# The main stage's list is made with durations, ways and one transfer queue read from a trace

## The chip, the core and the metric

The kernel runs on one core of one Trainium2 chip. The metric is device time in microseconds (us) of that core; a kernel's time is the median of its runs. TensorE is PE, VectorE is DVE, ScalarE is ACT, GpSimd is POOL; SyncE is SP, which here only issues transfers (ACT issues some as well). Two clocks occur for TensorE, 2.4 GHz (granted share 1.00) and 1.2 GHz (0.50).

## What is computed

Three layers follow each other: a decayed linear attention, a mixture of eight experts whose weights come from eight rounds of row and column normalisation, and a bilinear block. The two last make up the main stage.

```python
# x: (3072, 384), from the attention
P = np.exp(x @ w_gate - max)
for _ in range(8):
    P /= P.sum(1, keepdims=True) + 1e-09
    P /= P.sum(0, keepdims=True) + 1e-09
    P *= N / E
for e in range(8):
    out += P[:, e:e+1] * (np.maximum(x @ w1[e], 0.0) @ w2[e])   # w1[e]: 384x1024
y = ((out @ w_a) * (out @ w_b)) @ w_out                         # w_a: 384x1536
```

## The kernel before

Every float32 operand of a matmul is split into a high and a low part, and a product is three matmuls (high by high, high by low, low by high). The kernel has two stages, each with its own list of operations. The first (attention, the first expert for most rows) ends about 421 us into the span and is not touched. The second, the main stage, goes in six phases: three for the experts and three for the bilinear block, each with 1024 rows of `x`.

A phase is a row of *jobs*. The front of a job multiplies by the first weight, in a scheme with 15 products of sums instead of 18 plain ones: each is one group of three 128x512 matmuls (line 998) into a PSUM bank of `pG` (two banks) or `pF` (three banks). ACT copies a bank out to a buffer `z` ("keep"), or DVE adds or subtracts it into a `z`; there are 19 such buffers, handed out in turn while the program is written, so that the same operation always has the same buffer, in both kernels. ACT and POOL or DVE then make the high and low parts into `er`. The back of a job multiplies these by the second weight (line 368, 128x384 matmuls, 3 or 6 in an operation, three banks `pR`), and DVE adds each result into `acc`.

Beside this stand transfers: weights already split come back in three pieces (`w<-wfmoe`, `w<-wfout`), go out once as a whole (1920 KB, `wfmoe<-w`, `wfout<-w`), and `er<-w2d` brings the second weight. The 64-bit weights of the bilinear block are converted on DVE in seven small operations (lines 311 to 319) and written out by ACT (`wd<-z`, line 968). Where an expert phase ends, `acc` is transposed on PE (line 1126), copied to `z`, and written out by ACT (`x2d<-z`).

What sets the order of the instructions is a list scheduler, the class `Plan`. Each operation is added with a priority, an engine, a cost in us, and the buffers that it reads and writes. `Plan.order` lets time pass: each engine in turn takes, of the operations whose inputs are reckoned ready, the one with the lowest priority number; PE first prefers the kind (512 or 384 columns) that it has, until it has stayed `STAY` us with it. What is ready is reckoned so: the cost of the producer, and then, to another engine, a fixed gap (0.4 us here, 1.5 us to SP; 0.13 us on the same engine), and for a transfer a fixed `late` (3 us for a store, 5 us for a load). No transfer waits for another in this reckoning. The result is an order for each engine, which the chip follows strictly: an engine stands still until the next instruction's inputs are there. A POOL operation and those DVE operations that are marked "+" share a port in the list.

Of the kernel before, what the change touches and what calls it, by code (L numbers as in the profile page):

```python
# [84 lines left out]
class Plan:  # L85
# [11 lines left out]
    SWITCH = .02  # L97

    def __init__(self, gap=GAP, hold=GAP, same=SAME, over=0.0, ranked=False, early=0, slack=None, port=False, stay=0.0):
        self.port, self.shared, self.stay, self.kind = port, set(), stay, {}  # L100
        self.ranked, self.early, self.slack = ranked, early, slack or gap
        self.gap, self.hold, self.same, self.over = gap, hold, same, over
        self.ops = []
        self.last = {}

    def add(self, prio, eng, cost, reads, writes, fn, late=0.0, fill=False, kind=0):
        n = len(self.ops)
        self.kind[n] = kind
        if self.port and eng in ("POOL", "DVE+"):
            self.shared.add(n)  # L110
        eng = eng.rstrip("+")
        cost -= self.over if eng in ("DVE", "ACT") else 0.0
        deps = set()
        for key in reads:
            w, r = self.last.setdefault(key, (None, []))
            if w is not None:
                deps.add(w)
            r.append(n)
        for key in writes:
            w, r = self.last.get(key, (None, []))  # L120
            deps.update(x for x in r if x != n)
            if w is not None:
                deps.add(w)
            self.last[key] = (n, [])
        self.ops.append((prio, eng, cost, deps, fn, late, fill))
# [5 lines left out]
    def order(self, share):  # L131
# [67 lines left out]
                    todo.setdefault(self.ops[u][1], []).append(u)  # L199
        return made  # L200


@with_exitstack
def kernel(
# [36 lines left out]
    S_COST, X_COST = (.1, .0026), .9  # L241
    LATER = 8.0
    LATER_PE = 600
    STAY = 1.2
    SPREAD = 2000
    W_STEP = SPREAD // 3
    LAG = 100
# [39 lines left out]
    xd = [spill.tile([KD, 128, NT], F32, name=f"x{n}d") for n in (1, 2)]  # L287
# [14 lines left out]
    count = {"raw": 0, "h": 0, "w2": 0, "l": 0}  # L302
# [120 lines left out]
    PE, DVE, ACT, POOL, SP = "PE", "DVE", "ACT", "POOL", "SP"  # L423
    plan = Plan(same=.1, over=.07, ranked=True, early=2000, slack=.8)
# [503 lines left out]
    TPG = 2 * TB // 128  # L928
    plan = Plan(.4, 1.5, port=True, stay=STAY)
    used.update(F=0, R=0)  # L930
# [232 lines left out]
    for n, (ph, u, blocks, ab) in enumerate(jobs):  # L1163
        kind, g = phases[ph]
        base = n - u
        if u == 0:
            if ph:
                more = l_of + (stage_of if ph != 3 else []) + (raw_of if ph not in (1, 3) else [])
# [19 lines left out]
        end = n + 1 == len(jobs) or jobs[n + 1][0] != ph  # L1188
# [10 lines left out]
            first = False  # L1199
    assert not later  # L1200
    with tc.manual_schedule():
        for fn in plan.order(0.0):
            fn()  # L1203


# [38 lines left out]
```

## Time and profile before

| what | value |
|---|---|
| median of 3 runs | 2188.34 us (2185.81 to 2189.74) |
| profiled execution, its own time | 2187.57 us |
| its span in the profile | 2185.8 us |
| PE busy | 2159.0 us (99%) |
| DVE, ACT, POOL busy | 1610.4, 942.2, 910.4 us |
| granted clock, mean | 0.998 |

A matmul's record reaches from its start to the modelled end of its last column, and the next one starts before that: a busy PE is therefore one that always has the next matmul, not one at its peak. What PE can lose is read from its waits, from the granted clock, and from the distance between the starts of matmuls.

### The profile page before, as it was taken

What the parts mean: (1) busy time and instruction counts of PE and PEld (TensorE: products, weight loads), DVE (VectorE), ACT (ScalarE), POOL (GpSimd) and SP (SyncE); (2) the same over time, 40 slices, a digit from 0 to 9 for tenths busy, and PEclk for the clock granted to TensorE, in tenths of its full rate; (3) what the DMA queues carried; (4) which work ended last, traced back from release to release, by engine and by line L of the source; (5) the groups of instructions that cost most, each with busy time, mean ns of one, the idle gap of its engine ahead of it and who ended that gap; (6) DMA issues with size and microseconds to landing.
All of it is one profiled execution on the core that took longest, in us unless ns stands there. A gap on an engine that the chain in (4) does not pass through costs nothing.

```text
span 2185.8 us, 41932 instructions
## 1 busy us (share of the span) xinstructions
PE 2159.0 (99%) x15933; PEld 1961.6 (90%) x15933; DVE 1610.4 (74%) x2888; ACT 942.2 (43%) x1779; POOL 910.4 (42%) x924
## 2 busy tenths in 40 slices
PE   8999999999999999999999999999999999999999
PEld 8999999989999999898999988999999888888888
DVE  7878888387878778676787697677776866866755
ACT  3544454454444445433334344433343545533331
POOL 2212121378876664431222255433222577634322
PEclk9999999999999999999999999999999999999999
DMA  6556653456765558875454466666443555787552
GB/s 138 112 118 147 174 122 80 140 201 214 253 245 188 208 187 302 288 250 186 141 173 157 158 225 235 219 218 215 165 163 127 185 203 193 283 284 255 173 173 73
DMA packets 318346, 413.43 MB, mean 189 GB/s; under 512 B 146880, under 2 KB 207936, under 8 KB 314688
## 3 DMA queue, kind: packets, MB, share of 16 engines
q1 hardware_dynamic: 302832, 393.97, 56.0%
q10 hardware_dynamic: 15312, 16.78, 2.2%
q8 instruction: 125, 2.05, 0.4%
q14 instruction: 77, 0.63, 0.1%
HBM read 279.33 MB, written 126.62 MB: 186 GB/s over the span
## 4 chain that ended last, share of the span: by engine, by line
PE 93%; DVE 3%; DMA 2%; SPq 1%; ACT 0%; issue 0%; POOL 0%; ACTq 0%; DVEq 0%
PE pR L368 39%; PE pG L998 27%; PE pF L998 10%; PE pM L356 4%; PE pM L368 3%; PE pT L482 1%; PE pA L525 1%; PE pO L638 1%; PE pA L537 1%; PE pO L610 1%; PE pA L569 1%; PE pO L644 1%; PE pA L580 1%; DVE z L1203 1%; PE pO L682 1%; PE pM L729 0%
## 5 line engine op out<-in xcount | busy, mean ns | idle before, releaser
L368 PE MATMUL pR<-er 128*128 128x384 f32 x5052 | 976.2, 336 | 2.9 <-DVE acc L1203 2.7
L368 PEld LDWEIGHTS pR<-er 128*128 128x128 f32 x5052 | 897.9, 188 | 55.2 <-DVE acc L1203 3.0
L1203 POOL TENSOR_TENSOR er<-z,er 128x512 fp32r<-128x512 f32 x221 | 299.3, 1367 | 659.6 <-ACT er L1203 512.8
L1203 ACT ACTIVATE z<-pG 128x512 f32<-128x512 f32 x474 | 282.8, 599 | 658.6 <-PE pG L998 578.2
L1203 DVE SCALAR_TENSOR_TENSOR acc<-pR,prob,acc 128x384 f32<-128x384 f32 x504 | 305.2, 612 | 194.4 <-PE pR L368 192.8
L998 PE MATMUL pG<-xsh,w 128*128 128x512 f32 x1134 | 431.4, 394 | 5.9 <-ACT z L1203 5.8
L1203 ACT ACTIVATE er<-z 128x512 fp32r<-128x512 f32 x420 | 248.8, 625 | 143.4 <-PE pR L368 107.9
L1203 DVE TENSOR_TENSOR z<-pF,z 128x512 f32<-128x512 f32 x324 | 221.3, 687 | 93.6 <-PE pF L998 70.3
L998 PE MATMUL pG<-er,w 128*128 128x512 f32 x972 | 278.8, 395 | 1.2 <-DVE z L1203 0.8
L998 PEld LDWEIGHTS pG<-xsh,w 128*128 128x128 f32 x1134 | 212.7, 188 | 42.1 <-ACT z L1203 8.1
L1203 DVE TENSOR_TENSOR z<-z,pG 128x512 f32<-128x512 f32 x243 | 166.2, 685 | 84.7 <-PE pG L998 81.2
L998 PE MATMUL pG<-xsl,w 128*128 128x512 f32 x567 | 223.8, 395 | 0.0
L998 PEld LDWEIGHTS pG<-er,w 128*128 128x128 f32 x972 | 180.0, 188 | 32.8 <-DVE z L1203 3.7
L708 POOL TENSOR_TENSOR er<-l,er 128x256 fp32r<-128x256 f32 x84 | 71.7, 854 | 281.0 <-ACT l L706 249.5
L1203 DVE SCALAR_TENSOR_TENSOR er<-z,er 128x512 fp32r<-128x512 f32 x171 | 171.6, 1014 | 6.2 <-ACT er L1203 5.2
L1203 POOL TENSOR_TENSOR stage<-stage 128x128 f32<-128x128 f32 x325 | 158.9, 521 | 38.9 <-DMA stage<-in_moe_w_dram 28.9
L1203 DVE TENSOR_TENSOR z<-pG,z 128x512 f32<-128x512 f32 x174 | 119.9, 689 | 67.3 <-PE pG L998 64.5
L1203 POOL TENSOR_TENSOR w<-stage,w 128x768 fp32r<-128x768 f32 (+2 forms) x75 | 124.1, 1662 | 43.4 <-ACT w L1203 38.8
L998 PE MATMUL pF<-er,w 128*128 128x512 f32 x486 | 139.0, 394 | 1.4 <-DVE z L1203 1.4
L326 POOL TENSOR_TENSOR er<-raw,er 128x384 fp32r<-128x384 f32 (+1 forms) x82 | 94.5, 1157 | 98.5 <-ACT er L324 84.6
L998 PE MATMUL pF<-xsh,w 128*128 128x512 f32 x324 | 126.9, 393 | 0.0
L998 PEld LDWEIGHTS pG<-xsl,w 128*128 128x128 f32 x567 | 106.3, 188 | 10.7
(166 smaller groups left out, 2594.2 us busy)
## 6 DMA issues: line engine op xcount, KB each, us to landing
er<-w2d SPq DMA_DIRECT2D x138, 384.0 KB, 4.5
wfmoe<-w SPq DMA_DIRECT2D x19, 1920.0 KB, 7.8
w<-wfmoe SPq DMA_DIRECT2D x38, 768.0 KB, 5.2
w2d<-er SPq DMA_DIRECT2D x69, 384.0 KB, 4.0
w<-wfmoe SPq DMA_DIRECT2D x38, 640.0 KB, 4.9
w<-wfmoe SPq DMA_DIRECT2D x38, 512.0 KB, 4.3
wfout<-w SPq DMA_DIRECT2D x8, 1920.0 KB, 7.5
raw<-in_moe_w_dram SPq DMA_DIRECT2D x64, 192.0 KB, 2.9
```

The source lines that it names most:

```text
L326: plan.add(prio + 1, "POOL", S_COST[0] + m * S_COST[1], [gk, key], [key], lambda: nc.gpsimd.tensor_tensor(out=lj, in0=got, in1=f32(hj), op ...
L356: nc.tensor.matmul(out=ps, lhsT=a[:, kk, fs], rhs=b[:, kk, :], start=(i == 0), stop=(i == 3 * KD - 1),)
L368: nc.tensor.matmul(out=ps, lhsT=a[:, off:off + 128], rhs=b, start=(start and i == 0), stop=(stop and i == n - 1))
L482: nc.tensor.transpose(ps[0:R, p * 128:p * 128 + 128], src[:, p * 128:p * 128 + R], ident)
L525: nc.tensor.matmul(out=A0[o:o + 64, w, :], lhsT=pct(bk)[r, g, :], rhs=pct(bq)[r, g, :])
L537: nc.tensor.matmul(out=A1[o:o + 56, 0, w, :].rearrange("j (b e) -> j b e", e=8), lhsT=pct(k3)[r, g, 0:56], rhs=qv[r, g, :, 1, :])
L569: nc.tensor.matmul(out=A1[o:o + 48, 1, w, :].rearrange("j (b e) -> j b e", e=16), lhsT=pct(k3)[r, g, 0:48], rhs=qv[r, g, :, 1, :])
L580: nc.tensor.matmul(out=A1[o:o + 32, 0, w, :], lhsT=pct(k3)[r, g, 0:32], rhs=pct(q3)[r, g, 32:64])
L610: nc.tensor.matmul(out=ps[64 * hd:64 * hd + m, p * D:(p + 1) * D], lhsT=kn[64 * c:64 * c + 64, p * R + 64 * hd:p * R + 64 * hd + m], rhs=b ...
L708: op(POOL, .76, [f"hh{ft}", kf], [f"hl{ft}"], lambda hh=hh, hl=hl, hf=hf: nc.gpsimd.tensor_tensor(out=hl, in0=hf, in1=f32(hh), op=ALU.subt ...
L998: nc.tensor.matmul(out=ps, lhsT=a[:, slot], rhs=b, start=(new and i == 0), stop=(i == 2), skip_group_check=not new)
L1203: fn()
```

## The change

A second scheduler, `Plan.timed`, makes the main stage's list. It picks as `order` does, but counts with tables: `TAKES` has for each engine and reckoned cost the distance from start to start, `COLUMNS` and `AFTER` that of a matmul by its columns and its place in a run, `WAY` the way from each engine to the next one. Transfers from SP and ACT go through one queue, by bytes. `STAY` goes from 1.2 to 1.8. No operation is added or taken out, and the buffers of each stay the same. The list is called as `plan.timed(.03, .3)`: 0.03 us on top of each way, 0.3 us on top of a landing.

```diff
-    STAY = 1.2
+    STAY = 1.8
-        for fn in plan.order(0.0):
+        for fn in plan.timed(.03, .3):
             fn()
+    WAY = {"PE": .205, "DVE": .115, "ACT": .125, "POOL": .085}
+    COLUMNS = {512: .2267, 384: .1733, 256: .12}
+    AFTER = {512: (3.7, 6.7, 6.7, -1.2, 4.2, 8.7, 2.5, 5.0, 3.3, 0.0), 384: (-2.5, 3.7, 6.2, 2.5, 3.7, .8, 0.0),
+        "DVE": {.62: .528, .56: .467, .68: .602, .69: .603, .7: .603, .93: .91, 1.0: 1.016, .204: .22, .255: .28, .3: .24, .383: .3},
+        "ACT": {.6: .52, .45: .387, .49: .387, .521: .414, .612: .53, .737: .635, .863: .735, .37: .263, .47: .395, .25: .27},
+    DMA_WAY, DMA_RATE, DMA_PIECE = 1.93, 400e3, .001
+    def moves(self, n):
+        _, eng, cost, _, _, late, _ = self.ops[n]
+        key, cost, kb = self.key[n], round(cost, 3), 1024
+        if eng == "ACT":
+            return (256 * kb, 128) if key[:2] == "xd" else (128 * kb, 128)
+        if cost == .45:
+            return (1920 * kb, 128) if key[:2] == "wf" else (128 * kb * {"0": 6, "1": 4, "2": 5}[key[-1]], 256)
...
+            at, eng = best
+            n = min((n for n in todo[eng] if ready[n] <= at + 1e-9),
+                    key=lambda n: (eng == "PE" and (self.kind[n] == now) != (run < self.stay), prio[n]))
+            todo[eng].remove(n)
+            cost, late = round(self.ops[n][2], 3), self.ops[n][5]
+            if n in self.shared:
+                at = max(at, port - .03)
...
+                for _ in range(count):
+                    takes += self.COLUMNS[cols] + .001 * more[min(place, len(more) - 1)]
+                    place += 1
+            else:
+                takes = self.TAKES.get(eng, {}).get(cost, cost)
...
+            if n in self.shared:
+                port = max(port, at + takes)
...
+            free[eng] = end = at + takes
+            made.append(self.ops[n][4])
+            dma = eng == "SP" or (eng == "ACT" and late > 0)
+            if dma:
+                size, pieces = self.moves(n)
+                queue = max(end + self.DMA_WAY - .03, queue) + size / self.DMA_RATE + pieces * self.DMA_PIECE
+                end = queue + .03
+            for u in users[n]:
+                to = self.ops[u][1]
+                way = 0.0 if dma or (eng == to and eng != "SP") else self.WAY.get(eng, 0.0) + near
+                ready[u] = max(ready[u], end + way + (far if dma or to == "SP" else 0.0))
```

The lists differ on every engine, but most operations move by a few places. Three of them are needed below.

**Place 1, ACT** (some 1029 us into the span before): the store of a converted piece, `wd0_104<-z7_6478`, and the next operation that overwrites the same buffer `z7`. Before:

```order
L1203 ACTIVATE er_92<-z8_6479 128x512
L1203 ACTIVATE er_92<-z2_6473 128x512
L1203 ACTIVATE er_92<-z5_6476 128x512
L968 DMA wd0_104<-z7_6478 128x256
L1203 ACTIVATE z7_6478<-pG1_6464 128x512
L1203 ACTIVATE z11_6482<-pG0_6463 128x512
```

And now:

```order
L1065 DMA wd0_104<-z7_6478 128x256
L1300 ACTIVATE z6_6477<-pG0_6463 128x512
L1300 ACTIVATE er_92<-z8_6479 128x512
L1300 ACTIVATE er_92<-z2_6473 128x512
L1300 ACTIVATE er_92<-z5_6476 128x512
L1300 ACTIVATE z1_6472<-pG0_6463 128x512
L1300 ACTIVATE z17_6488<-z17_6488 128x512
L1300 ACTIVATE z12_6483<-pG0_6463 128x512
L1300 ACTIVATE z0_6471<-z0_6471 128x512
L1300 ACTIVATE er_92<-z17_6488 128x512
L1300 ACTIVATE er_92<-z15_6486 128x512
L1300 ACTIVATE z14_6485<-pG0_6463 128x512
```

The store stood right ahead of the operation that overwrites its source; now eleven activations stand between, and `z11` and then `z7` come behind the last of these rows.

**Place 2, PE**, at the same time: the matmuls ahead of the `pG` product of job parts `xsh_6496`, which needs the bank that `z11` is copied from. Before:

```order
L998 MATMUL pF_6467<-er,w_84 128x512 x3
L368 MATMUL pR_6468<-er 128x384 x6
L368 MATMUL pR_6469<-er 128x384 x6
L998 MATMUL pF_6465<-xsh_80,w_85 128x512
L998 MATMUL pF_6465<-xsl_81,w_85 128x512
L998 MATMUL pF_6465<-xsh_80,w_85 128x512
L998 MATMUL pF_6467<-er,w_84 128x512 x3
L368 MATMUL pR_6470<-er 128x384 x6
L368 MATMUL pR_6468<-er 128x384 x6
L998 MATMUL pG_6463<-xsh_6496,w_84 128x512
```

And now:

```order
L1095 MATMUL pG_6463<-xsh_6494,w_84 128x512
L1095 MATMUL pG_6463<-xsl_6495,w_84 128x512
L1095 MATMUL pG_6463<-xsh_6494,w_84 128x512
L1095 MATMUL pG_6464<-xsh_74,w_85 128x512
L1095 MATMUL pG_6464<-xsl_75,w_85 128x512
L1095 MATMUL pG_6464<-xsh_74,w_85 128x512
L1095 MATMUL pF_6467<-er,w_84 128x512 x3
L465 MATMUL pR_6470<-er 128x384 x6
L465 MATMUL pR_6468<-er 128x384 x6
L1095 MATMUL pG_6463<-xsh_6496,w_84 128x512
```

A run of six matmuls with 512 columns has become one of nine. Over the main stage the 3645 matmuls with 512 columns stand in 514 runs (593 before), most of six or nine, and the 5010 with 384 columns in 502 (577 before).

**Place 3, ACT**, some 1793 us into the span before: the three stores of transposed rows at the end of the third phase, and the operations that overwrite `z8`, `z2` and `z4` again. Before:

```order
L1203 DMA x2d_97<-z8_6479 128x512
L1203 DMA x2d_97<-z2_6473 128x512
L1203 ACTIVATE z4_6475<-pR1_6469 128x512
L1203 ACTIVATE w10_84<-stage_86 128x640
L1203 DMA x2d_97<-z4_6475 128x512
L1203 ACTIVATE er_92<-z0_6471 128x512
L1203 ACTIVATE er_92<-z12_6483 128x512
L1203 ACTIVATE z8_6479<-pG1_6464 128x512
L1203 ACTIVATE z4_6475<-pG0_6463 128x512
L1203 ACTIVATE z2_6473<-pG1_6464 128x512
```

And now:

```order
L1300 DMA x2d_97<-z8_6479 128x512
L1300 ACTIVATE z2_6473<-pR0_6468 128x512
L1300 DMA x2d_97<-z2_6473 128x512
L1300 ACTIVATE z4_6475<-pR1_6469 128x512
L1300 DMA x2d_97<-z4_6475 128x512
L1300 ACTIVATE er_92<-raw0_87 128x384
L1300 ACTIVATE w10_84<-stage_86 128x640
L1300 ACTIVATE er_92<-z0_6471 128x512
L1300 ACTIVATE z8_6479<-pG1_6464 128x512
L1300 ACTIVATE z2_6473<-pG1_6464 128x512
L1300 ACTIVATE z4_6475<-pG0_6463 128x512
```

The store of `z8` goes out one activation earlier, and `z4`, the last to be stored, is now overwritten last.

## Rows read from the trace of the kernel before

**Rows 1.** The page: engine share, and the costliest group (mean ns behind the comma).

```profile
PE   2159.0 (99%) x15933; PEld 1961.6 (90%) x15933; DVE 1610.4 (74%) x2888; ACT 942.2 (43%) x1779; POOL 910.4 (42%) x924
...
L368 PE MATMUL pR<-er 128*128 128x384 f32 x5052 | 976.2, 336 | 2.9 <-DVE acc L1203 2.7
```

**Rows 2.** PE's waits from 421 us on: total us, times, longest.

```profile
PE pG L998 <- ACT z L1203: 5.8, 4, 2.0
PE pR L368 <- DVE acc L1203: 2.7, 1, 2.7
PE pR L1126 <- DVE acc L1203: 2.5, 2, 1.9
PE pF L998 <- DVE z L1203: 1.4, 1, 1.4
PE pR L778 <- DVE prob L769: 1.2, 2, 1.0
PE pG L998 <- DVE z L1203: 0.8, 3, 0.5
PE pR L356 <- ACT l L722: 0.3, 1, 0.3
PE pG L998 <- DVE er L1203: 0.3, 1, 0.3
PE pR L368 <- ACT acc L1203: 0.2, 1, 0.2
```

**Rows 3.** Windows behind two waits: PE, PEld, DVE, ACT, POOL busy, PEclk, DMA share, GB/s.

```profile
1037.30:1042.00 4.70, 4.65 (x16) 4.38 (x17) 1.93 (x4) 2.15 (x4) 2.59 (x2) 0.66 0.26 96
...
1284.70:1288.00 3.30, 3.22 (x8) 2.79 (x9) 2.13 (x5) 0.63 (x1) 0.62 (x1) 0.50 0.57 193
```

**Rows 4.** Timeline, 1026 to 1039 us: start, us, engine, line, tiles; idle time in brackets.

```profile
1026.31 0.52 SPq L1203 DMA_DIRECT2D w<-wfmoe  x1
...
1028.37 0.39 PE L998 MATMUL pG<-xsh,w 128*128 128x512 f32 x1
...
1028.78 0.34 ACTq L968 DMA_DIRECT2D wd<-z  x1
...
1029.76 2.25 PE L368 MATMUL pR<-er 128*128 128x384 f32 x12
...
1031.85 0.39 PE L998 MATMUL pF<-xsh,w 128*128 128x512 f32 x1
...
1033.23 2.25 PE L368 MATMUL pR<-er 128*128 128x384 f32 x12
...
1036.21 1.08 ACT L1203 ACTIVATE z<-pG 128x512 f32<-128x512 f32 x2 [8.22 <-DVE acc L1203]
...
1037.35 0.50 PE L998 MATMUL pG<-xsh,w 128*128 128x512 f32 x1 [1.86 <-ACT z L1203]
```

**Rows 5.** The chain that ended last, 1020 to 1045 us, its longest piece.

```profile
1028.78 7.34 DMA wd<-z
```

**Rows 6.** Timeline, 1790 to 1808 us.

```profile
1793.25 0.43 SPq L1203 DMA_DIRECT2D wfout<-w  x1
...
1793.53 0.81 ACTq L1203 DMA_DIRECT2D x2d<-z  x2
...
1801.13 0.60 ACT L1203 ACTIVATE z<-pG 128x512 f32<-128x512 f32 x1 [4.09 <-DMA x2d<-z]
...
1801.78 0.50 PE L998 MATMUL pG<-xsh,w 128*128 128x512 f32 x1 [2.01 <-ACT z L1203]
...
1805.59 0.50 PE L998 MATMUL pG<-xsh,w 128*128 128x512 f32 x1 [1.26 <-ACT z L1203]
```

**Rows 7.** Transfers by line: issues, KB each, median us to landing.

```profile
wfout<-w SPq DMA_DIRECT2D x8, 1920.0 KB, 7.5
...
wd<-z ACTq DMA_DIRECT2D x36, 128.0 KB, 2.7
x2d<-z ACTq DMA_DIRECT2D x18, 256.0 KB, 5.7
```

**Rows 8.** Timeline, 1274 to 1287 us.

```profile
1281.54 1.39 DVE L317 TENSOR_TENSOR z<-z 128x256 f32<-128x256 f32 x1
...
1284.12 0.60 DVE L1203 SCALAR_TENSOR_TENSOR acc<-pR,prob,acc 128x384 f32<-128x384 f32 x1
...
1284.78 1.33 PE L368 MATMUL pR<-er 128*128 128x384 f32 x3 [2.66 <-DVE acc L1203]
```

More of the change, by code (lines that the diff above doesn't have):

```diff
@@ L99, in __init__ @@
     def __init__(self, gap=GAP, hold=GAP, same=SAME, over=0.0, ranked=False, early=0, slack=None, port=False, stay=0.0):
-        self.port, self.shared, self.stay, self.kind = port, set(), stay, {}
+        self.port, self.shared, self.stay, self.kind, self.key = port, set(), stay, {}, {}
         self.ranked, self.early, self.slack = ranked, early, slack or gap
@@ L108, in add @@
         self.kind[n] = kind
+        self.key[n] = next(iter(writes), "")
         if self.port and eng in ("POOL", "DVE+"):
@@ L200, in order @@
         return made
+    ENGINES = ("PE", "DVE", "ACT", "POOL", "SP", "clock")
+    WAY = {"PE": .205, "DVE": .115, "ACT": .125, "POOL": .085}
+    RUNS = {.681: (512, 3), 1.362: (512, 6), .522: (384, 3), 1.044: (384, 6), .53: (384, 3), 1.06: (384, 6),
+            .36: (256, 3), .72: (256, 6), 1.08: (256, 9)}
+    COLUMNS = {512: .2267, 384: .1733, 256: .12}
+    AFTER = {512: (3.7, 6.7, 6.7, -1.2, 4.2, 8.7, 2.5, 5.0, 3.3, 0.0), 384: (-2.5, 3.7, 6.2, 2.5, 3.7, .8, 0.0),
+             256: (2.0,), "pause": (6.0, 6.2, 3.3, 7.5, 3.3, 2.5, 2.5, 2.0, 0.0)}
@@ new lines @@
+    TAKES = {
+        "PE": {.2: .117, .33: .245, .35: .2, .69: .713},
+        "DVE": {.62: .528, .56: .467, .68: .602, .69: .603, .7: .603, .93: .91, 1.0: 1.016, .204: .22, .255: .28, .3: .24, .383: .3},
+        "ACT": {.6: .52, .45: .387, .49: .387, .521: .414, .612: .53, .737: .635, .863: .735, .37: .263, .47: .395, .25: .27},
+        "POOL": {.46: .417, 1.026: .977, 1.252: 1.256, 1.29: 1.256, 1.54: 1.522, 1.828: 1.81, .76: .72},
+        "SP": {.36: .46, .38: .47, .4: .42, .42: .4, .45: .615, 1.2: 1.23, 2.4: 2.5},
+    }
@@ new lines @@
+    DMA_WAY, DMA_RATE, DMA_PIECE = 1.93, 400e3, .001
[6 more added lines that the diff above has]
+            return (1920 * kb, 128) if key[:2] == "wf" else (128 * kb * {"0": 6, "1": 4, "2": 5}[key[-1]], 256)
+        if cost == .38:
+            return 384 * kb, 128
+        if key[:2] == "pb":
+            return 256 * kb, 512
+        return (256 * kb if cost == .4 and key[:2] != "sg" else 192 * kb), 128
@@ new lines, in timed @@
+    def timed(self, near, far, shift={}):
+        left, users, ready = [], [[] for _ in self.ops], [0.0] * len(self.ops)
+        todo = {eng: [] for eng in self.ENGINES}
+        prio = [o[0] + shift.get(n, 0) for n, o in enumerate(self.ops)]
+        for n, o in enumerate(self.ops):
+            left.append(len(o[3]))
+            for d in o[3]:
+                users[d].append(n)
+            if not o[3]:
+                todo[o[1]].append(n)
+        free, port, queue, run, now, made = dict.fromkeys(self.ENGINES, 0.0), 0.0, 0.0, 0.0, 0, []
+        width, place, paused = 0, 0, False
+        while any(todo.values()):
+            best = None
+            for eng, ns in todo.items():
+                if ns:
+                    soon = min(ready[n] for n in ns)
+                    at = soon if eng == "clock" else max(free[eng], soon)
+                    if best is None or at < best[0]:
+                        best = (at, eng)
+            at, eng = best
[5 more added lines that the diff above has]
+                at = max(at, port - .03)
+            if eng == "PE" and cost in self.RUNS:
+                cols, count = self.RUNS[cost]
+                if width != cols:
+                    width, place, paused = cols, 0, False
+                if at > free["PE"] + .04:
+                    place, paused = 0, True
+                more = self.AFTER["pause" if paused else cols]
+                takes = 0.0
+                for _ in range(count):
[3 more added lines that the diff above has]
+                takes = self.TAKES.get(eng, {}).get(cost, cost)
+                if eng == "ACT" and late and cost == .45:
+                    takes = .42
+                if eng == "PE":
+                    width, place, paused = 0, 0, False
+            if n in self.shared:
+                port = max(port, at + takes)
+            if self.kind[n]:
+                run = takes + (run if self.kind[n] == now else 0.0)
+                now = self.kind[n]
+            free[eng] = end = at + takes
[9 more added lines that the diff above has]
+                ready[u] = max(ready[u], end + way + (far if dma or to == "SP" else 0.0))
+                left[u] -= 1
+                if not left[u]:
+                    todo[to].append(u)
+        return made
```

## Prediction

> **What bounds it now.** I first read the engine shares: PE is busy for 99% of the span [rows 1], and no other engine for more than 74%. So the main stage ends when PE has got through its matmuls, and a change of order can win or lose three things only: PE's waits, its clock, and the distance between its starts.
>
> I read the waits next, for the main stage alone [rows 2]. The nine rows add up to 5.8 + 2.7 + 2.5 + 1.4 + 1.2 + 0.8 + 0.3 + 0.3 + 0.2 = 15.2 us, in 16 waits. Few, then, and long: there is no steady shortage, but single places where the list was mistaken. A wait costs more than its row shows, since it is counted from the end of a matmul's record. A 384-column record lasts 0.336 us on average [rows 1], while 12 such matmuls go from 1029.76 to 1031.85, that is 0.174 us each [rows 4]. So a wait costs another 0.16 us, 2.6 us over 16.
>
> Third, the clock. Behind two waits, of 1.86 and 2.66 us, there is a stretch at a lower grant: 0.66 on average over 4.70 us, and 0.50 (the 1.2 GHz level) over 3.30 us [rows 3]. That is 4.70 x 0.34 + 3.30 x 0.50 = 3.25 us lost.
>
> In all 15.2 + 2.6 + 3.25 = 21 us hang on waits: 1% of the time, and the most that better order can return there.
>
> **The hops.** The old list adds 0.4 us for every way to another engine. At 1801.13 ACT takes 0.60 us, and PE starts at 1801.78, 0.05 us behind [rows 6]: 0.65 us, where the old list counts 0.6 + 0.4 = 1.0, and the new one 0.52 + 0.125 + 0.03 = 0.675. DVE's `acc` at 1284.12 takes 0.60, and PE starts 0.06 us behind it [rows 8]; the old list counts 0.62 + 0.4 = 1.02, the new one 0.528 + 0.115 + 0.03 = 0.673. So the old list sees chains of hops as half as long again as they are, and the new one is within a few hundredths. Too long a reckoning does not make PE wait by itself; it makes the list prefer the wrong work. But it also was a reserve of 0.35 us at each hop, and this is gone: the main danger, to which I come back.
>
> **The landings.** Here the old list errs to the other side, and this ends waits. It counts 0.45 + 3.0 us for each store by ACT. The `wd<-z` store issued at 1028.78 took 7.34 us [rows 5], and the `z` that it read is overwritten by the next activation, which therefore stood still, with PE behind it: 1.86 us [rows 4]. Its median is 2.7 us [rows 7]; this one went out behind loads like that at 1026.31 [rows 4]. The two stores from 1793.53 on went out 0.28 us behind a store of 1920 KB, whose median landing is 7.5 us [rows 6, 7]. The first had landed at 1801.13, 7.6 us behind its issue, when ACT went on; PE's waits of 2.01 and 1.26 us follow [rows 6].
>
> The new table by hand: 1920 KB at 400,000 bytes per us are 4.9 us, so the big store keeps the queue until about 1793.25 + 0.6 + 1.9 + 4.9 + 0.1 = 1800.8, and the small store, another 0.65 + 0.13 us, lands at 1801.6: 0.5 us from what the row shows. The table therefore describes what happened there. The Trainium skill, page "DMA: Bandwidth & Descriptors", section "Queues, rings and completion order", speaks against one queue: each transfer engine takes a packet from every row that has work in turn, and SP and ACT own one row each. By that, the small store would not have stood behind all of the large one. The row of 7.6 us is nearer to the queue; I go by it, and keep the other as a rival.
>
> **The sum**, against the profiled execution's own 2187.57 us (0.77 us under the median of the runs).
>
> Place 1: the store now goes out eleven activations earlier than the overwriting of its buffer (the order rows of ACT). Only `er` parts and copies that PE feeds lie between, at least 11 x 0.6 = 6.6 us of ACT's time by the activation's 0.60 [rows 6]. The wait goes, with its restart and its slow stretch: 1.86 + 0.16 + 1.60 = -3.6 us. If the cover were gone, the 1.86 would come back.
>
> Place 3: the three stores and the three overwritings stand about as before; whether the 1920 KB store goes ahead of the small ones is a matter of some tenths of a microsecond on SP, which the order can't tell. If it goes behind, both waits go: 3.27 + 0.32 = 3.6 us. If ahead, they stay or grow by a microsecond or two, since PE has less in between. I take half: -1.8 us (ends -3.6 and +2).
>
> The 2.66 us behind DVE: small operations of the conversion took 1.39 us [rows 8] where the old list counts 0.38 and the new one 0.3, because POOL was on the port at that moment. Both lists know the port, neither knew this collision. The order moves, so this coincidence goes, with its slow stretch: 2.66 + 0.16 + 1.65 = 4.5 us; another like it may appear anywhere. I take half: -2.2 us (ends -4.5 and +2).
>
> The other 12 waits, 15.2 - 5.13 - 2.66 = 7.4 us and 1.9 us of restarts, lie mostly at phase ends and in the first 45 us, where little other work stands ready for PE. Right hops help to choose it, but do not create it: half again, -4.6 us (ends -9.3 and 0).
>
> The joints: the stretch at 1028.37 has six 512-column matmuls in 1.39 us, that at 1031.85 in 1.38: 0.231 and 0.230 each, and the run of 12 with 384 columns 0.174 [rows 4]. Whether a run of nine goes faster no row of mine shows. With 79 and 75 runs fewer, and a few hundredths of a microsecond for a joint at most, the bounds are 0 and -2; I take 0, as the two stretches are alike.
>
> New waits by the thin reserve: +1.5 us, some seven of 0.05 + 0.16 us (ends 0 and +20, below).
>
> Sum: -3.6 - 1.8 - 2.2 - 4.6 + 1.5 = -10.7 us, so 2176.9 for an execution like the profiled one, **2177.6 us** for the median.
>
> **Rivals.**
>
> *No measurable change: the waits move.* The list takes each landing as certain to 0.3 us. The rows of one kind scatter by more: `wd<-z` has a median of 2.7 us and an instance of 7.34 [rows 5, 7]. A list that plans an operation for the very moment at which its input is reckoned to land puts PE behind each late load. Eight such waits of 1.2 us with restart give +10, and 2187.6. For it: the reserve of loads falls from 5 us to what the bytes give. Against it: the one case that I could count by hand came out 0.5 us late, on the safe side.
>
> *Slower: the thin reserve.* A reserve of 0.02 to 0.07 us is used up wherever an operation runs late by a tenth, and PE, which can't pass over a matmul, stands still with 0.16 us on top: 0.2 to 0.25 us each time. It takes 10.7 + 1.5 + 4.4 = 16.6 us, some 70 such places among the 1016 runs of PE, to end above 2192.7; with 100, about 2199. For it: DVE operations on the port last three times as long as counted [rows 8]. Against: durations off the port repeat to a few hundredths, and three banks `pR` and five others lie between.
>
> *The queue is wrong.* If SP's and ACT's transfers go side by side, the reckoned landings of stores are too late and those of loads wrong, and the terms of places 1 and 3 fall away: 2177.6 + 5.4 = 2183.0. Against it stands the 7.6 us row.
>
> **How the numbers follow.** About 0.2%, 4.4 us, is what a measurement of this kernel tells from no change. My forecast has 0.70, with a range of its own from 2168 to 2184; the wrong queue 0.06, just on the faster side; no change 0.14; slower 0.10. So faster 0.76, same 0.14, slower 0.10. The low end is that all 21 us and the joints go, 2165.3, which I cut a little; the high end takes in most of the second case: 2167 to 2188.
>
> **What would show it.** After the change, PE's waits in the main stage add up to 6 to 10 us, with at most one above 2 us; no wait follows a `wd<-z` landing; the granted clock is at or near 1.00 throughout; the mean distances of matmuls are as before. I am wrong if there are many short waits on ACT or DVE (more than 40), if one port collision brings a slow stretch back, or if PE waits for loads of `w` or `er`.

## The result, and the profile after

The changed kernel takes 2206.14 us (median of 6 runs, 2203.91 to 2209.95), beside 2189.31 us for the kernel before. The ratio is 1.0079 (95% interval 1.0068 to 1.0090): some 17 us slower, where some 11 faster were forecast.

The engine shares answer to [rows 1] first. PE is busy for 13.6 us more with the same 15933 matmuls; the other engines have nearly what they had.

```profile
PE   2172.6 (98%) x15933; PEld 1968.5 (89%) x15933; DVE 1615.2 (73%) x2888; ACT 947.9 (43%) x1779; POOL 913.4 (41%) x924
```

Then PE's waits in the main stage, the view of [rows 2]:

```profile
PE pG L1095 <- DVE z L1300: 9.8, 9, 2.8
PE pG L1095 <- ACT z L1300: 6.9, 5, 3.3
PE pR L465 <- DVE acc L1300: 4.2, 6, 2.7
PE pF L1095 <- POOL xsl L1300: 0.4, 1, 0.4
```

They add up to 21.3 us in 21 waits, where it was 15.2 in 16. The kind has changed: waits on ACT's copies have grown by a microsecond, those on DVE's sums `z` from 0.8 + 1.4 to 9.8 us.

What DVE itself waited for (the view of waits, DVE, main stage):

```profile
DVE z L408 <- DMA z<-in_moe_w_out_dram: 7.7, 6, 2.5
DVE z L408 <- DMA z<-in_moe_w_b_dram: 7.0, 7, 2.1
DVE z L408 <- DMA z<-in_moe_w_a_dram: 5.3, 4, 1.9
```

These are the loads of the weights to be converted: 20.0 us in 17 waits. The same view of the kernel before has no such row. The old list reckoned their landing with a `late` of 8 us, the constant `LATER`, and not with the 5 us that I named; the new one counts bytes, plus 0.3 us. One such place in the chain that ended last, 955 to 964 us (start, us, what):

```profile
949.06 8.06 DMA z<-in_moe_w_a_dram
...
957.22 0.30 DVE z L408
...
957.55 1.41 DVE z L410
...
958.98 0.30 DVE z L411
...
959.30 1.47 DVE z L412
...
960.79 0.71 DVE z L414
961.51 0.61 DVE z L1300
...
962.17 0.96 PE pG L1095 x3
```

The load takes 8.06 us. DVE stands still until it lands; then two of the small operations take 1.41 and 1.47 us, while POOL works on `er` beside them (from 957.23 and from 959.19); and the sum `z` for PE comes behind all of it. PE waits 1.34 us.

The clock, the view of [rows 3]: five stretches at half the clock in the changed kernel, and the first of them in the same place of the kernel before.

```profile
19.00:29.20 10.20, 10.00 (x111) 8.94 (x112) 6.43 (x13) 0.80 (x4) 1.27 (x1) 0.50 0.58 128
916.70:920.10 3.40, 3.40 (x9) 2.64 (x8) 2.90 (x6) 1.12 (x2) 2.30 (x2) 0.50 0.14 49
1363.80:1370.60 6.80, 5.55 (x19) 4.87 (x20) 5.84 (x15) 2.31 (x4) 1.28 (x1) 0.50 0.27 104
1770.00:1773.40 3.40, 3.40 (x11) 2.91 (x10) 1.13 (x3) 2.32 (x5) 2.64 (x5) 0.50 0.85 329
1821.20:1824.60 3.40, 3.06 (x9) 2.78 (x10) 0.00 (x0) 1.38 (x3) 1.34 (x4) 0.50 0.05 20
```

```profile
19.00:29.20 10.20, 9.59 (x200) 8.72 (x200) 8.63 (x21) 1.70 (x6) 1.69 (x2) 1.00 0.64 140
```

The first lies in the stage that the change doesn't touch and costs this execution some 5 of the 20.2 us by which the two profiled spans differ (2206.0 and 2185.8); the medians are 17 apart. The main stage alone, from PE's first `pG` matmul on (421.4 and 425.5 us), is 16 us longer. The four other stretches, 17.0 us at half the clock, cost 8.5 us; the two of before cost 3.25 [rows 3]. These are single executions, but the others agree: the mean granted clock is 0.994 over the six runs of the changed kernel and 0.996 over the 121 of the kernel before beside the experiments.

The last part is the pace. Behind six matmuls with 512 columns a run of twelve with 384 takes 2.09 us from start to start, behind nine it takes 2.11 (the timeline of PE, changed kernel):

```profile
1036.02 0.85 PE L1095 MATMUL pG<-er,w 128*128 128x512 f32 x3
1036.71 2.25 PE L465 MATMUL pR<-er 128*128 128x384 f32 x12
1038.80 0.39 PE L1095 MATMUL pG<-xsh,w 128*128 128x512 f32 x1
...
1040.19 0.85 PE L1095 MATMUL pF<-er,w 128*128 128x512 f32 x3
1040.88 2.27 PE L465 MATMUL pR<-er 128*128 128x384 f32 x12
1042.99 0.39 PE L1095 MATMUL pG<-xsh,w 128*128 128x512 f32 x1
```

The run at 1036.71 stands behind the six from 1035.33 on, the one at 1040.88 behind the nine from 1038.80 on. Counted in its order, the new list has 118 runs of twelve behind nine: 118 x 0.02 = 2.4 us, if all go like these.

Together: waits +6.1, five more restarts at 0.16 are +0.8, half clock 8.5 - 3.25 = +5.2, pace +2.4: 14.5 of the 16 us.

What is missing can be found in starts that are late by too little to make a wait row, because a matmul's record overlaps the next start. I count, from the starts in the traces at full clock, matmuls without a wait row that start over 0.03 us later than the usual 0.231 us (512 columns) or 0.174 us (384) after the one before. The kernel before has 35 of them, 4.2 us in all, and the changed kernel 62, 6.9 us; about half come right behind a wait.

### The profile page after: what moved, and what is told of

It is laid out like the page before. It is cut to its first block, busy times and chain, and to the rows that moved or that the text cites. A ratio compares the mean times of both kernels' runs of the same rounds, so it can differ in the third digit from the quotient of the medians.

```text
span 2206.0 us, 41926 instructions
## 1 busy us (share of the span) xinstructions
PE 2172.6 (98%) x15933; PEld 1968.5 (89%) x15933; DVE 1615.2 (73%) x2888; ACT 947.9 (43%) x1779; POOL 913.4 (41%) x924
## 4 chain that ended last, share of the span: by engine, by line
PE 87%; DVE 6%; DMA 4%; POOL 1%; ACT 1%; issue 1%; SPq 1%; ACTq 0%; DVEq 0%; POOLq 0%
PE pR L465 35%; PE pG L1095 25%; PE pF L1095 9%; PE pM L453 4%; PE pM L465 3%; DVE z L1300 2%; PE pT L579 1%; PE pA L622 1%; DMA z<-in_moe_w_out_dram 1%; PE pO L735 1%; PE pA L634 1%; PE pO L707 1%; PE pA L666 1%; PE pO L741 1%; DVE acc L1300 1%
## 5 line engine op out<-in xcount | busy, mean ns | idle before, releaser
L1095 PEld LDWEIGHTS pG<-er,w 128*128 128x128 f32 x972 | 179.4, 189 | 42.2 <-DVE z L1300 15.1
L1300 DVE SCALAR_TENSOR_TENSOR er<-z,er 128x512 fp32r<-128x512 f32 x171 | 156.2, 924 | 18.0 <-ACT er L1300 16.1
L1300 ACT ACTIVATE z<-z 128x512 f32<-128x512 f32 x114 | 71.9, 631 | 116.0 <-DVE z L1300 114.8
```

The costliest lines, as they stand in the source:

```text
L1095: nc.tensor.matmul(out=ps, lhsT=a[:, slot], rhs=b, start=(new and i == 0), stop=(i == 2), skip_group_check=not new)
```

## The experiments

What is compared throughout is the ratio to the kernel before on the same chip; in microseconds it is (ratio - 1) x 2189. Theory A: the lost reserve of the conversion's loads. B: the hops without reserve. C: the run length. D, formed later: the spare time in the old operation costs.

| run | against before | 95% interval | us |
|---|---|---|---|
| changed kernel | 1.0079 | 1.0068 to 1.0090 | +17.3 |
| e1_conv_reserve | 1.0059 | 1.0047 to 1.0071 | +12.9 |
| e2_hop_reserve | 1.0029 | 1.0017 to 1.0041 | +6.3 |
| e4_stay12 | 1.0042 | 1.0030 to 1.0054 | +9.2 |
| e5_before_short | 1.0018 | 1.0004 to 1.0031 | +3.9 |
| e3_stay_alone | 0.9989 | 0.9981 to 0.9998 | -2.4 |
| e6_hop_stay | 1.0006 | 0.9996 to 1.0017 | +1.3 |
| e7_hop_stay_conv | 1.0031 | 1.0018 to 1.0044 | +6.8 |
| e8_before_gap02 | 0.9973 | 0.9963 to 0.9984 | -5.9 |
| e9_occupancy | 1.0023 | 1.0012 to 1.0035 | +5.0 |
| e10_conv_measured | 1.0048 | 1.0029 to 1.0067 | +10.5 |
| e11_near04 | 1.0038 | 1.0024 to 1.0051 | +8.3 |
| e12_far35 | 1.0036 | 1.0024 to 1.0048 | +7.9 |
| e13_pitch_alone | 0.9995 | 0.9985 to 1.0005 | -1.1 |
| e14_queue_alone | 0.9972 | 0.9962 to 0.9983 | -6.1 |
| e15_before_gap041 | 1.0032 | 1.0020 to 1.0045 | +7.0 |
| e17_before_gap021 | 1.0014 | 1.0004 to 1.0024 | +3.1 |
| e16_pitch_way | 1.0103 | 1.0085 to 1.0120 | +22.5 |
| e18_queue_gap041 | 0.9978 | 0.9966 to 0.9990 | -4.8 |

### The first round: giving back one thing

**e1_conv_reserve**

```diff
-                end = queue + .03
+                end = max(queue + .03, end + late) if late > 6.0 else queue + .03
```

> The changed kernel; only the reckoned landing of the conversion's loads (the ones with 8 us of late in the old list) is put back to at least 8 us behind the issue. Theory A (the conversion's lost reserve is the cause): DVE waits for these loads fall from 20.0 us in 17 waits to under 3, the five PE waits behind them (1.6, 2.0, 1.3, 2.8, 2.7 us) and two or three of the stretches at half clock go, and the time is 2187 to 2194. Theory B (the hops of 0.03 us are too thin, the loads are only where it shows): DVE waits for loads fall too, but PE's waits come up elsewhere and the time stays at 2200 to 2206.

+12.9 us. No wait of DVE for these loads is left, and PE still waits for DVE (PE's waits of e1, three of six rows):

```profile
PE pG L1095 <- DVE z L1300: 8.5, 11, 1.6
PE pR L465 <- DVE acc L1300: 6.1, 7, 2.3
PE pG L1095 <- ACT z L1300: 4.4, 5, 2.2
```

One `z` wait, of 1.57 us, ends at 1320.26. DVE and then POOL ahead of it, in e1's timeline:

```profile
1314.57 1.32 DVE L411 TENSOR_SCALAR z<-z 128x256 int32<-128x256 int32 x1
1315.93 1.40 DVE L412 SCALAR_TENSOR_TENSOR z<-z,z 128x256 f32<-128x256 uint32 x1
1317.37 1.38 DVE L414 TENSOR_TENSOR z<-z 128x256 f32<-128x256 f32 x1
1318.67 0.94 DVE L1300 TENSOR_TENSOR er<-stage,er 128x512 fp32r<-128x512 f32 x1
1319.53 0.68 DVE L1300 TENSOR_TENSOR z<-pG,z 128x512 f32<-128x512 f32 x1
```

```profile
1314.45 1.30 POOL L1300 TENSOR_TENSOR l<-l,l 128x512 f32<-128x512 f32 x1 [0.19 <-DMA l<-x2d]
1315.71 2.76 POOL L1300 TENSOR_TENSOR er<-z,er 128x512 fp32r<-128x512 f32 x2
```

The first conversion ends at 1315.89 and the third at 1318.75, 0.14 and 0.28 us behind ends of POOL's (1315.75 and 1318.47); the second, at 1317.33, ends near the middle of POOL's pair. They take 4.1 us together, where by the means of their 36 instances in this kernel it is 0.419 + 0.577 + 0.569 = 1.57. So no late load is needed for DVE to be late; POOL beside it is enough. A, as the whole cause, falls.

**e2_hop_reserve**

```diff
-        for fn in plan.timed(.03, .3):
+        for fn in plan.timed(.2, .3):
```

> The changed kernel with 0.2 us instead of 0.03 us on top of each way between engines, everything else as changed. Theory A: the loads are planned as before, so 2200 to 2210. Theory B: the short waits of 0.2 to 0.4 us (eleven, 3 us in all) go and the long ones shrink: 2185 to 2196.

+6.3 us: by the ratio (2195) inside B's range, by the median of 2198.1 us 2 us over it. A gain of 11 on the changed kernel, so B gets most of what it claimed, if the draw (below) is left aside.

**e4_stay12**

```diff
-    STAY = 1.8
+    STAY = 1.2
```

> The changed kernel with STAY at 1.2 as before, the tables as changed. If the longer runs on PE starve the other engines (theory C) the time goes to 2195 or lower; theories A and B say 2200 to 2210, as the waits come from the reckoning and not from the run length.

+9.2 us: by the median, 2201.5 us, at the low end of what A and B expect, by the ratio (2198) just below it; no support for C.

**e5_before_short** (the kernel before)

```diff
-    LATER = 8.0
+    LATER = 4.0
```

> The kernel before with one number changed: the conversion's loads are reckoned with 4 us of late instead of 8 (4.8 us with the gap, near the median landing of 4.4 to 4.8). Theory A: DVE now waits for such loads here too, in some 10 to 20 of 60 cases, and the time rises to 2196 to 2208. Theory B: the wide hops of the old list remain, so the time stays within 5 us of 2189.

+3.9 us. The 2197.2 us lie at the low end of A's range, but the kernel before took 2191.3 on that chip, so the loss is within the 5 us of B. DVE does wait for the loads here, 8.0 + 6.5 + 3.7 = 18.2 us, nearly as much as in the changed kernel:

```profile
DVE z L311 <- DMA z<-in_moe_w_out_dram: 8.0, 5, 3.3
DVE z L311 <- DMA z<-in_moe_w_a_dram: 6.5, 5, 2.7
DVE z L311 <- DMA z<-in_moe_w_b_dram: 3.7, 2, 2.3
```

So idle time of DVE for loads, nearly as much as in the changed kernel, goes with a quarter of its loss in this one list. It is where the mistake shows, but not most of what it costs.

### The second round: one part in the old list, several undone in the new one

**e3_stay_alone** (the kernel before)

```diff
-    STAY = 1.2
+    STAY = 1.8
```

> The kernel before (old reckoning) with STAY at 1.8 instead of 1.2: the run-length part of the change by itself, 510 and 495 runs instead of 593 and 577. Theory C (longer runs cost by themselves: 384-column runs behind nine matmuls of 512 columns took 22 ns more per run of twelve, and PE's banks are drained in bursts): 5 to 9 us slower than before in the same job. Theory B (the thin hop does it): within 3 us of before.

-2.4 us. C falls: longer runs don't make the kernel slower by themselves. The pace is paid here too, with 98 runs of twelve behind nine in this trace; but PE's waits add up to 11.2 us, 4 less than before.

**e6_hop_stay**

```diff
-    STAY = 1.8
+    STAY = 1.2
...
-        for fn in plan.timed(.03, .3):
+        for fn in plan.timed(.2, .3):
```

> The new tables with 0.2 us on top of each way and STAY at 1.2. If the thin hop and the run length add up (theories B and C: -11 and -8 of +17 us), it stands within 3 us of before. If they remove the same waits, it stays 4 to 8 us above.

+1.3 us, as if both added up. With 0.2 us at each hop and the old run length the tables are, in this list, no worse than the old reckoning.

**e7_hop_stay_conv** (as e6_hop_stay, with the line of e1_conv_reserve)

> As the one above, and the conversion's loads reckoned with 8 us again. Theory A's share, some 4 us by the two runs so far, comes on top: 0 to 5 us below before. If the loads matter only where hops are thin, no difference to the run above.

+6.8 us: a reserve that should only help made it 5.5 us slower. No theory so far had room for this, and it raised the question of how far a list scatters.

**e8_before_gap02** (the kernel before)

```diff
-    plan = Plan(.4, 1.5, port=True, stay=STAY)
+    plan = Plan(.2, 1.5, port=True, stay=STAY)
```

> The kernel before with 0.2 us instead of 0.4 for each way between engines in the old reckoning; tables, landings and STAY as before. Theory B: a thin reserve costs in the old list too, 5 to 12 us slower than before. If only the mixture of the new tables does harm, within 3 us.

-5.9 us, outside both readings. B in its plain form falls: in the old list a hop of 0.2 us costs nothing.

### The third round: neighbours, and spare time on the engines

**e9_occupancy**

```diff
+            held = max(cost, takes) if eng in ("DVE", "ACT", "POOL") and not late else takes
             if n in self.shared:
-                port = max(port, at + takes)
+                port = max(port, at + held)
...
-            free[eng] = end = at + takes
+            free[eng], end = at + held, at + takes
```

> The changed kernel (hops 0.03, STAY 1.8), but DVE, ACT and POOL are held, in the reckoning, for the old costs (0.70 instead of 0.603 us for a DVE operation, 0.60 instead of 0.52 for an ACT copy); when a result is ready is counted as in the changed list. Theory D (what the old list had and the new one lost is spare time on the engines, which the collisions on the port use up): 2188 to 2196, with PE's waits on DVE at half. If only the hop matters (theory B): 2200 to 2206 as changed.

+5.0 us, within D's range. But D's other sign did not come: PE's waits on DVE, of which this is the longest row, add up to 15.7 us, not to half of the 14.0 of the changed kernel. So it is no clear support for D.

```profile
PE pR L466 <- DVE acc L1301: 7.8, 3, 6.5
```

**e10_conv_measured**

```diff
-        "DVE": {..., .204: .22, .255: .28, .3: .24, .383: .3},
+        "DVE": {..., .204: .376, .255: .42, .3: .46, .383: .56},
```

> The changed kernel with one group of the table corrected: the small DVE operations of the conversion are counted with the mean durations that the trace of the kernel before shows (0.38 to 0.56 us, collisions on the port included) instead of 0.22 to 0.30. If the undercounted conversion is what makes DVE late (a narrow form of theory D): 2192 to 2200. Otherwise 2201 to 2210.

+10.5 us: in the range of the narrow form of D, but no better than the two neighbours that follow, so it shows nothing.

**e11_near04** (`plan.timed(.04, .3)`)

> The changed kernel with 0.04 instead of 0.03 us on top of each way: no theory gives this a cost or a gain. How far the time moves shows what a reshuffled list does by chance; if the thin reserve has a steady price it stays within 4 us of the changed kernel, 15 to 20 us above before.

+8.3 us, 9 less than the changed kernel, where within 4 was expected.

**e12_far35** (`plan.timed(.03, .35)`)

> The changed kernel with 0.35 instead of 0.30 us on top of each landing: a second neighbour, again without a cost or a gain of its own. Within 4 us of the changed kernel if the price is steady; anywhere between 0 and 20 us above before if the changed list was an unlucky draw.

+7.9 us, as the second reading had it. Two edits without a meaning move the time by 9 us. The changed list was an unlucky draw of its kind, whose three draws have a mean of (17.3 + 8.3 + 7.9) / 3 = 11.2.

PE's waits add up to 16.0 us in e11 and to 15.1 us in e12, no more than the 15.2 of the kernel before, and still both are 8 us slower. What they have more of are late starts without a wait row, 66 and 70 (8.0 and 7.9 us, against 4.2), and the pace of longer runs. So the loss that the three lists share hardly shows in PE's wait rows.

### The last rounds: the scatter of the old list, and its parts

**e15_before_gap041** and **e17_before_gap021** (the kernel before, `Plan(.41, ...)` and `Plan(.21, ...)`)

> The kernel before with a gap of 0.41 instead of 0.40 us: a neighbour without a meaning. It shows how far the old list scatters; within 4 us of before if it does not, up to 8 us off if the old list was a lucky draw.

> The kernel before with a gap of 0.21 us, a neighbour of the run with 0.20 that was 5.9 us faster than before. If the shorter gap is a gain of its own, 3 to 8 us faster again; if that run was a lucky draw, within 4 us of before on either side.

+7.0 and +3.1 us, both as the reading with a lucky draw had it. The old list scatters as much: 0 and +7.0 with the long hop, -5.9 and +3.1 with the short one, mean +1.1. Between the two kinds of list remains 11.2 - 1.1 = 10 us; the other 6 to 7 of the 17 are the draw. With three and four draws, each kind spread over 9 to 13 us, this division is rough by several us.

**e13_pitch_alone** (in `order`, STAY 1.2, hop 0.4)

```diff
+            if part and eng in ("DVE", "ACT", "POOL"):
+                cost = .42 if eng == "ACT" and late else self.TAKES[eng].get(round(cost, 3), cost)
```

> The kernel before with one part of the change: DVE, ACT and POOL operations are counted with the new table of pitches, while gaps (0.4), landings, PE's pitch and STAY stay old. Theory D (lost spare time on the engines): 5 to 12 us slower than before, with PE's waits on DVE up. If the pitches are harmless: within 4 us.

-1.1 us: the shorter operation costs (the pitches, from start to start) are harmless while a hop has 0.4 us.

**e16_pitch_way** (as e13_pitch_alone, and the hops)

```diff
+                far = self.WAY[eng] + .03 if part and eng in self.WAY and not late and self.ops[u][1] != "SP" else far
```

A hop now has 0.115 to 0.235 us, by the engine that it starts from. An operation that follows one on its own engine no longer has 0.13 us added either.

> The old list with the new pitches of DVE, ACT and POOL and the new ways (plus 0.03 us) together; landings, PE's pitch and STAY stay old. If the loss comes where both kinds of spare time are gone (theories B and D together): 7 to 15 us above before. If it comes from the landings, the pitch of PE or STAY in the new reckoning: within 6 us of before.

+22.5 us, the slowest of all and beyond the 7 to 15 expected, with landings, PE's pitch and STAY as in the kernel before. The first row of PE's waits in e16, and the like rows of e13 and of e8:

```profile
PE pG L1098 <- DVE z L1303: 16.6, 21, 1.9
```

```profile
PE pG L1097 <- DVE z L1302: 4.6, 7, 1.4
```

```profile
PE pG L998 <- DVE z L1203: 2.8, 3, 2.0
```

Short costs alone: 7 such waits. Hops of 0.2 us alone: 3. Short costs with still shorter hops: 21, and 87 late starts without a wait row, where e13 has 42 and e8 37. Between e13 and e16 lie 23.6 us, well beyond the scatter of 9 us, though e16 is one list without a neighbour. Hops as short as in e16 with the old costs were not run.

**e14_queue_alone** (in `order`, everything else old)

```diff
+            if dma:
+                size, pieces = self.moves(n)
+                queue = max(at + cost + self.DMA_WAY - .03, queue) + size / self.DMA_RATE + pieces * self.DMA_PIECE
+                late = queue + .03 - at - cost
...
+                far = .3 if dma else self.hold if self.ops[u][1] == "SP" else self.slack if ever else self.gap
```

> The kernel before with one part of the change: landings from one queue by bytes plus 0.3 us, everything else old. Theory A in its wide form (landings without reserve cost): 5 to 12 us slower, with DVE waits for the conversion's loads as in the changed kernel (20 us). If the queue is the good part of the change, as predicted: 3 to 7 us faster.

-6.1 us, although DVE waits 8.9 us for the conversion's loads in it. PE's waits on ACT's copies, 5.8 us before [rows 2], and DVE's for the loads:

```profile
PE pG L1100 <- ACT z L1305: 0.7, 1, 0.7
```

```profile
DVE z L413 <- DMA z<-in_moe_w_out_dram: 4.0, 5, 1.4
DVE z L413 <- DMA z<-in_moe_w_a_dram: 3.1, 3, 1.9
DVE z L413 <- DMA z<-in_moe_w_b_dram: 1.8, 3, 1.0
```

**e18_queue_gap041** (the same with `Plan(.41, ...)`)

> The old list with landings from the queue, as in the run that was 6 us faster than before, and a gap of 0.41 as in the neighbour that was 7 us slower. If the queue is a gain of its own: 4 to 10 us faster than that neighbour, so 3 above to 3 below before. If the 6 us were a draw: anywhere from 4 below to 10 above before.

-4.8 us; against its own neighbour without the queue, e15, that is 11.8 us less. Both numbers are a little beyond what either reading allowed, on the side of the queue. Two draws, both faster than before and 6 and 12 us under their counterparts: the queue is probably a gain. Its size is not settled, since e8_before_gap02 without it is as fast. Nor is the way settled: e14 has lost the waits on ACT's copies, but e18 has the wait at place 3 again, of 3.3 us:

```profile
PE pG L1100 <- ACT z L1305: 4.0, 2, 3.3
```

These two and e8_before_gap02, and by 2.4 us e3_stay_alone, beat both kernels; no list with the new hops does.

## Why the prediction was wrong

**Hops.** The lengths were read rightly, and so was the danger. The step that failed is the term of new waits, +1.5 us, and its price: I priced a used-up reserve as 0.2 to 0.25 us at each place, which takes 70 places for a loss. In fact 21 waits make 21.3 us, where 6 to 10 us were forecast for all of PE's waits. A late operation on DVE doesn't delay one hop; it holds all that stands behind it in DVE's order, and a conversion beside POOL can add a microsecond for each of its operations. The small late starts that I had priced are there too, 62 instead of 35, but they make only +2.7 us.

What the old list had against lateness was in two places: 0.4 us at the hop (0.13 on the same engine), and costs longer than the pitch (0.70 instead of 0.603). I weighed the first and took the second for mere inaccuracy. e16 shows that without both the loss comes, with landings, run length and PE's pitch as before; e13 shows that the long hop alone is enough. That long costs alone are enough is shown for hops down to 0.2 us only (e8, e17). The rival "the thin reserve", to which I gave 0.10, is what came about, but not with more than 40 short waits: with half as many long ones, and with the other sign that I had named, half the clock beside a port collision (the stretch from 1363.8 us).

**Landings.** Place 1 went as argued: the `wd<-z` store goes out at 1032.56 in the changed kernel and lands at 1034.94; its buffer is overwritten from 1048.76 on, and PE's rows from 1019 to 1053 hold no idle time. Place 3 went to its bad end. The 1920 KB store was issued at 1811.85; the chain that ended last, 1808 to 1826 us, and PE's timeline there:

```profile
1812.39 0.61 ACT z L1300
...
1813.02 7.85 DMA x2d<-z
...
1820.89 0.61 ACT z L1300
```

```profile
1817.59 0.69 PE L465 MATMUL pR<-er 128*128 128x384 f32 x3
1821.54 0.80 PE L1095 MATMUL pG<-xsh,w 128*128 128x512 f32 x1 [3.26 <-ACT z L1300]
```

The first small store goes out at 1813.02, behind the large one, and lands 7.85 us later; ACT overwrites its buffer only then, and PE waits 3.26 us, as much as the 2.01 and 1.26 of before together [rows 6]. The term of -1.8 was 0. As a part, the queue's two lists lie 6 and 12 us under their counterparts (e14, e18), where I gave 5.4 to both places, but e18 has the same wait at place 3.

The rival "the queue is wrong" is right about the rows and wrong about the landing. In the kernel before, both rows moved at the same time while the large store ran, from 1796 to 1799.5 us (packets, MB, share; q1 is SP's row, q10 ACT's):

```profile
q1 hardware_dynamic: 88, 1.35, 92.8%
q10 hardware_dynamic: 76, 0.16, 11.4%
```

Nearly as many packets went on either row, some 15 KB each on SP's and 2 KB on ACT's. This agrees with the packet-wise turns of the Trainium skill's "DMA: Bandwidth & Descriptors" ("Queues, rings and completion order"). With such turns only 0.16 MB went on ACT's row beside 1.35 on SP's, and the store of 256 KB still landed 7.6 us behind its issue [rows 6]. In the changed kernel ACT's row moved nothing from the issue at 1813.02 until 1817 us, nearer to one queue. So the one queue was a fair reckoning of when these two small stores land, and not a description of how the rows share the engines.

**The other side of the landings** I had as a rival, "the waits move", with 5 us as the lost reserve of loads. For the conversion it was 8, on a line of the planner that I had not looked up. It makes 20.0 us of waits on DVE, but by e1, e5 and e14 they are not the main cost.

**The 2.66 us behind DVE.** "Another like it may appear": it did, at 1737 us, with 2.68 us; the term of -2.2 was 0.

**The other waits.** -4.6 us was a hope that right hops choose better work. 21.3 - 3.26 - 2.68 = 15.4 us in 19 waits stand against 7.4 in 12: +8.

**Clock and joints.** The clock was to be whole; four stretches made +5.2 us in the profiled execution. For the joints I set 0, with bounds of -2 and 0, and it was +2.4.

**The draw.** The range had no term for it. Some 6 to 7 of the 17 us come from no property of the change, by the few draws there are; the long waits on DVE are in good part the draw's, since e11 and e12 lose 8 us without more waits than before; the kernel with 0.04 for 0.03 measured +8.3, which is some 2197 and outside the range as well.

Left open: PE's pitch by shape was not tried alone; hops of 0.03 us over the way and the missing 0.13 us on the same engine were not tried with the old costs; of STAY in the new list (+9.2 with 1.2 against a mean of 11.2) nothing can be said beyond the scatter; and e2 and e9, each of which gives back one kind of spare time (+6.3, +5.0), lie below that mean by less than the scatter, so that the share of each is not settled.

## What to carry to other kernels

A planner's "wrong" numbers may be its reserve. Before replacing them by measured ones, ask for each what lateness it absorbs, keep as much elsewhere, and put the measured values in one kind at a time: here the landings were probably worth correcting, and the durations and hops could not both go to their measured values. Time two or three neighbours without a meaning before believing a single list: a difference under 9 us (0.4%) between two single lists said nothing here, however narrow the interval. And count late starts beside the waits: two lists with the old sum of waits were 8 us slower.

## What the runs showed of the hardware

A run of twelve matmuls with 384 columns takes 2.11 us behind nine with 512 columns and 2.09 behind six, with the same engine at the same clock (means of 117 and 63 such runs of the changed kernel). The conversion's operations on DVE (128x256) take 0.42 to 0.64 us on average in e1, and 1.3 to 1.4 in the stretch shown above beside POOL operations of 1.3 us. From 1796 to 1799.5 us of the kernel before, 76 packets of 2 KB on ACT's row went beside 88 of 15 KB on SP's, and the small store landed 7.6 us behind its issue, as late as the large one. And half-clock stretches came behind waits of 1.86 and 2.66 us before, behind 2.0, 2.8, 1.9 and 3.3 in the changed kernel, but not behind the one of 2.01 at 1799 us [rows 6] nor the one of 2.68 at 1737: length alone does not decide.
